# Re-timing the background transfers of a two-stage kernel: stores on GpSimd's queue, later weight casts, an earlier start

## The chip, the cores and the metric

The kernel runs on one core of a Trainium2 chip. The metric is device time in microseconds; quoted times are medians over several runs. The runs of one set were made on one chip, different sets on different chips, and times are compared only with runs of the kernel before on the same chip. A profile is one execution. "Gate end" below is the end of the last TensorE matmul of the first stage in the profile, counted from the start of the span.

## The reference, cut to what matters

```python
# gate loop: q, k, v, a_re, a_im are (4 batches, 8 heads, 768 steps, 48)
mag = np.sqrt(a_re * a_re + a_im * a_im)
scale = np.minimum(mag, 0.999) / (mag + 1e-06)
a_re_n, a_im_n = (a_re * scale, a_im * scale)
for t in range(S):
    ...   # S_re, S_im turned and shrunk by (a_re_n, a_im_n)
    S_re, S_im = (new_re + kv, new_im)
    y[:, :, t] = np.einsum('bhd,bhde->bhe', q[:, :, t], S_re)

# experts: x is y as 3072 rows of 384; 8 experts of 384 x 1024 x 384
logits = x @ w_gate + modality_bias[modality_id]
e_idx = np.argmax(logits, axis=1)
...       # gate_w is the softmax value of the chosen expert
h = np.maximum(x[mask] @ w1[e], 0.0)
out[mask] = gate_w[mask, None] * (h @ w2[e])
```

## The kernel before

The gate stage works on 24 units, one for each stretch of 128 steps of each batch, two units to a group. For a group, ScalarE and VectorE turn `a` into angles and moduli. For a unit, TensorE transposes Q and K, makes scores (`wp`), updates a state, makes outputs and turns them into rows. One loop runs the phases of several units in a software pipeline. A turn `w` belongs to one unit; negative turns fill the pipeline.

In the background, GpSimd's queue copies the experts' weights to bfloat16 in 16 "casts" of 768 KB output each. They are spread over the turns by hand. SyncE's queue carries everything else, in order: the loads of q, k, v and a; the stores of fractions (`f_scr`), moduli (`m_scr`) and rows (`x_rows`); the reloads of the fractions as carries (`cb`) and of the moduli (`mt`).

```python
    def moduli(x):
        ...
            nc.sync.dma_start(out=m_scr[n0:n0 + NG]..., in_=pm[L - 1:L, 0]...)
            mt = un.tile([C, NG, H], F32, name="mt", bufs=4)
            for c in range(2):
                nc.sync.dma_start(out=mt[c * D:(c + 1) * D], in_=m_scr[n0:n0 + NG].rearrange("i h d -> d i h"))
    ...
    phase(fractions, 0)
    phase(squares, 2)
    ...
    for w in range(-4, NU + 1):
        even = w % 2 == 0
        x = w // 2
        unit(values, w + 2)
        if even:
            phase(load_a, x + 6)
            phase(carries, x + 4)
            phase(fractions, x + 3)
        else:
            phase(load_qk, x + 3)
            hats(w + 3)
        unit(turned, w + 2)
        ...
        if w == 0:
            rt = make_router(ctx, ps, bank)       # loads the modality ids; VectorE compares them at once
        marks.append(chain[-1])
        if casts and w >= 0 and w % 3 != 2:
            cast = casts.pop(0)()                 # not before a mark two turns back
            tc.add_manual_dep(cast.ins, marks[-3].ins.name, ..., reason="spreads the casts over the turns")
```

After the gate stage come the router's last steps and the expert stage, which streams expert weights and does the two matmuls for up to 19 blocks of rows.

## Time and profile before

| measure, kernel before | value |
|---|---|
| median before the prediction, 3 runs | 396.49 us (395.16 to 397.88) |
| profiled execution, span | 392.2 us |
| scores of units 0, 2, 3, 5 start | 47.5, 68.6, 78.3, 96.6 us |
| scores of units 10 and 12 start | 145.9 and 171.8 us |
| gate end | 277.8 us |
| from there to the end of the span | 114.5 us |

The unit starts are read from TensorE's timeline. Where nothing disturbs it, a unit takes 9.75 us. So the table can be read as a sum: the ramp up to unit 5, the dip between units 10 and 12, a fixed pace, and the expert stage.

The waits of TensorE between 30 and 100 us (line waited for: total us, times, longest), which show the ramp hanging on ScalarE:

```profile
PE u L157 <- ACT tan L91: 14.7, 2, 9.7
PE wp L273 <- DVE f L180: 1.3, 2, 0.8
```

Second, GpSimd's timeline at 45 to 60 us (start, duration, what, and the idle time before it with what ended it). The first two casts start 7 us apart:

```profile
50.67 0.97 POOL L423 DMA_DIRECT2D w1b<-in_moe_w_dram  x1 [43.99 <-ACT off L91]
57.67 0.89 POOL L424 DMA_DIRECT2D w2b<-in_moe_w_dram  x1 [6.02 <-ACT sq L91]
```

The durations there are those of issuing. The page's list of transfers gives the landing: 7.6 us and 10.6 us after the issue, in the median. So the two overlap or touch, in the middle of the ramp.

### The profile page before, as it was taken

The page shows a single profiled execution, that of the slowest core. Times are in us where ns is not written, and L with a number is a line of the kernel's source. Part 1 is how long each engine was busy: PE and PEld are TensorE (multiplying, and loading weights), DVE is VectorE, ACT ScalarE, POOL GpSimd, SP SyncE. Part 2 cuts the span into 40 slices and gives each one's busy share as a digit, 9 for nine tenths or more (in the row PEclk, how much of TensorE's full clock was granted, in tenths as well). Part 3 has the DMA queues.
Part 4 walks back from the last instruction along what each step waited for, and adds up shares of the span by engine and source line. Part 5 has one row for each costly group of instructions (what it writes and reads, how often), then busy time and mean ns, then how long its engine had stood idle before and what let it go on. Part 6 is the DMA issues. An engine that isn't in the chain of part 4 may idle for free.

```text
span 392.2 us, 8756 instructions
## 1 busy us (share of the span) xinstructions
PE 328.1 (84%) x3381; PEld 269.9 (69%) x3381; DVE 259.0 (66%) x556; ACT 239.2 (61%) x386; POOL 79.6 (20%) x106
## 2 busy tenths in 40 slices
PE   0070949999999997899999999999407999999993
PEld 0030728788888886797979798999305777787772
DVE  2568797797969787997889789735632443443431
ACT  2859896989897978397979675352121333333331
POOL 5000010000000000000000011000045676776433
PEclk9996879999999999899999999999855999999999
DMA  9997599899899999979899993930169999999981
GB/s 145 187 152 173 91 163 184 125 195 195 150 222 159 184 166 217 185 126 147 184 181 186 153 160 64 185 69 13 30 245 365 404 404 413 405 407 406 411 357 40
DMA packets 173075, 80.89 MB, mean 206 GB/s; under 512 B 150387, under 2 KB 162152, under 8 KB 173034
## 3 DMA queue, kind: packets, MB, share of 16 engines
q1 hardware_dynamic: 158042, 59.97, 62.5%
q0 software_dynamic: 14992, 20.37, 26.5%
q8 instruction: 26, 0.43, 0.4%
q14 instruction: 15, 0.12, 0.1%
HBM read 85.75 MB, written 21.11 MB: 272 GB/s over the span
## 4 chain that ended last, share of the span: by engine, by line
PE 57%; ACT 11%; DMA 10%; issue 8%; POOL 4%; SPq 4%; DVE 4%; POOLq 0%; DVEq 0%; ACTq 0%
PE wp L273 9%; PE h_ps L702 7%; PE y_ps L713 6%; PE up L287 5%; PE xw L312 5%; PE yp L299 4%; DMA cb<-f_scr 4%; PE tQT L262 4%; PE yp L302 4%; PE tKT L262 4%; PE ls L207 4%; ACT sq L91 3%; PE u L157 3%; POOL out_dram L721 3%; ACT pm L91 2%
## 5 line engine op out<-in xcount | busy, mean ns | idle before, releaser
L157 PE MATMUL u<-tan,turn 128*128 128x384 f32 x48 | 24.4, 595 | 36.5 <-ACT tan L91 36.5
L273 PE MATMUL wp<-QT,KT 96*64 96x128 f32 x768 | 48.0, 278 | 1.7 <-DVE f L180 1.7
L273 PEld LDWEIGHTS wp<-QT,KT 96*64 96x64 f32 x768 | 42.2, 139 | 6.2 <-DVE f L180 2.7
L706 ACT ACTIVATE hT<-h_ps 128x512 bf16<-128x512 f32 x31 | 18.5, 597 | 45.6 <-PE h_ps L702 45.6
L702 PE MATMUL h_ps<-xgT,w1t 128*128 128x256 bf16 (+1 forms) x456 | 45.8, 259 | 0.0
L713 PE MATMUL y_ps<-w2t,hT 128*128 128x384 bf16 x248 | 43.5, 326 | 0.2 <-DVE hT L704 0.2
L702 PEld LDWEIGHTS <-w1t 128*128 128x128 bf16 x456 | 39.0, 100 | 5.9
L423 POOL DMA_DIRECT2D w1b<-in_moe_w_dram x8 | 5.9, 734 | 171.1 <-ACT off L91 86.3
L679 POOL DMA_INDIRECT xg<-x_rows,idx x31 | 30.0, 966 | 51.9 <-ACT idx L663 42.8
L157 PEld LDWEIGHTS u<-tan,turn 128*128 128x128 f32 x48 | 9.7, 230 | 41.2 <-issue 24.4
L721 POOL DMA_INDIRECT out_dram<-y_sb,idx x31 | 31.2, 1007 | 29.7 <-ACT y_sb L717 20.0
L299 PE MATMUL yp<-W,V 128*64 128x128 f32 x384 | 36.3, 277 | 0.0
L274 DVE TENSOR_TENSOR W<-wp,mask 128x512 f32<-128x512 f32 x48 | 32.3, 684 | 4.4 <-PE wp L273 4.3
L713 PEld LDWEIGHTS <-hT 128*128 128x128 bf16 x248 | 23.4, 98 | 14.1 <-DVE hT L704 0.3
L88 ACT ACT_TABLE_LOAD x25 | 32.1, 1283 | 1.2 <-PEq L800 0.8
L287 PEld LDWEIGHTS up<-V,Kh 128*96 128x96 f32 x320 | 29.5, 165 | 4.0 <-issue 2.7
L704 DVE TENSOR_SCALAR hT<-h_ps 128x512 bf16<-128x512 f32 x31 | 21.4, 692 | 16.0 <-PE h_ps L702 10.9
L302 PE MATMUL yp<-QT,state 96*48 96x128 f32 x320 | 31.1, 272 | 0.0
L287 PE MATMUL up<-V,Kh 128*96 128x48 f32 x320 | 30.4, 248 | 0.0
L263 ACT COPY KT<-tKT 96x512 f32<-96x512 f32 x48 | 25.8, 587 | 6.2 <-PE tKT L262 6.1
L304 ACT COPY yT<-yp 128x512 f32<-128x512 f32 x24 | 14.0, 585 | 22.7 <-PE yp L302 22.6
L312 PE MATMUL xw<-sel,yT 128*128 128x104 f32 x192 | 27.1, 285 | 0.0
(137 smaller groups left out, 653.3 us busy)
## 6 DMA issues: line engine op xcount, KB each, us to landing
w1t<-w1b SPq DMA_DIRECT2D x19, 768.0 KB, 12.0
w2t<-w2b SPq DMA_DIRECT2D x19, 768.0 KB
w1b<-in_moe_w_dram POOLq DMA_DIRECT2D x8, 768.0 KB, 7.6
w2b<-in_moe_w_dram POOLq DMA_DIRECT2D x8, 768.0 KB, 10.6
ab<-in_a_re_dram SPq DMA_DIRECT2D x24, 192.0 KB, 4.3
ab<-in_a_im_dram SPq DMA_DIRECT2D x24, 192.0 KB, 7.5
qk<-in_q_dram SPq DMA_DIRECT2D x24, 192.0 KB, 4.4
qk<-in_k_dram SPq DMA_DIRECT2D x24, 192.0 KB, 5.7
```

The lines of the kernel that those rows point to most:

```text
L88: then(nc.scalar.preload_act_table_set(name))
L157: nc.tensor.matmul(u, turn[:], tan[:, i], start=True, stop=False)
L262: nc.tensor.transpose(tp[:, i, :], src[:, h4 + i].rearrange("t c d -> t (c d)"), ident[:])
L273: nc.tensor.matmul(wp[u * 64:(u + 1) * 64, i, :], KT[:, h4 + i, u * 64:(u + 1) * 64], QT[:, h4 + i, :], start=True, stop=True)
L274: nc.vector.tensor_tensor(W[:, h4:h4 + 4], wp, mask[:, None, :].broadcast_to([L, 4, L]), Alu.mult)
L287: nc.tensor.matmul(up[:, h, :], Kh[:, h].rearrange("t c d -> t (c d)"), V[:, h, 0:D], start=True, stop=True)
L299: nc.tensor.matmul(yp[u * 64:(u + 1) * 64, j, :], V[:, 2 * j + u, :], W[:, 2 * j + u, :], start=True, stop=(g == 0))
L302: nc.tensor.matmul(yp[u * 64:u * 64 + D, j, :], old[:, 2 * j + u, :], QT[:, 2 * j + u, :], start=False, stop=True)
L312: nc.tensor.matmul(xw[:, j, :], yT[:, j, :], sel[:, j, :], start=True, stop=True)
L702: nc.tensor.matmul(h_ps[:, f, :], w1t[:, k, ff * 128:(ff + 1) * 128], xgT[:, k, :], start=(k == 0), stop=(k == KD - 1))
L713: nc.tensor.matmul(y_ps[:], hT[:, f, s * 128:(s + 1) * 128], w2t[:, f, :], start=(f == 0), stop=(f == NF - 1))
L721: sc = nc.gpsimd.indirect_dma_start(out=out, out_offset=bass.IndirectOffsetOnAxis(ap=idx[:, s, 1:2], axis=0), in_=y_sb[:], in_offset=None, ...
```

## The change

The intent is to keep TensorE from starving early in the gate stage: fewer weight casts while the loads are dense, no stores in front of loads in SyncE's queue, and the first units started one turn sooner. The diff, cut to its core:

```diff
-    Vs = [... for i in range(3)]
+    Vs = [... for i in range(4)]
...
-            nc.sync.dma_start(out=f_scr...)
+            nc.gpsimd.dma_start(out=f_scr...)
...
-            nc.sync.dma_start(out=m_scr...)
+            nc.gpsimd.dma_start(out=m_scr...)
...
-            for c in range(2):
-                nc.sync.dma_start(out=mt[c * D:(c + 1) * D], in_=m_scr...)
+    def decays(x):            # first half of mt, from memory
+            nc.sync.dma_start(out=mt[0:D], in_=m_scr...)
+    def decays2(x):           # second half, from the first, on the chip
+            nc.sync.dma_start(out=mt[D:C], in_=mt[0:D])
...
-        nc.sync.dma_start(out=x_rows...)
+        queue = nc.gpsimd if g < G - 1 else nc.sync
+        queue.dma_start(out=x_rows...)
...
-    phase(squares, 2)
+    with tc.issue_after(box["last"].ins):     # VectorE: after the first fractions
+        phase(squares, 2)
...
-        unit(values, w + 2)
+        n = w + 1 if w < 0 else w
+        unit(values, n + 2)
...      # likewise turned, inner, outer, hats, rows: n in place of w; each runs once
+            if w == -3:
+                hats(0)
...
+            if w < 0:
+                phase(sums, x + 2)
+                phase(moduli, x + 2)
...
-        if casts and w >= 0 and w % 3 != 2:
+        if casts and (w > 9 or w % 3 == 1 and w > 0):
```

More of the change, by code (lines that the diff above doesn't have):

```diff
@@ L72, in bank @@
         return flat.rearrange(f"p ({names}) -> p {names}", **{f"x{i}": s for i, s in enumerate(shape[1:])})
-    Vs = [un.tile([L, H, 64], F32, name=f"V{i}", bufs=1) for i in range(3)]
+    Vs = [un.tile([L, H, 64], F32, name=f"V{i}", bufs=1) for i in range(4)]
     for V in Vs:
@@ L185, in fractions @@
                 nc.vector.tensor_scalar(r[:, i], us[i], ROUND, -ROUND, Alu.add, Alu.add)
-                nc.vector.tensor_tensor(f[:, i], us[i], r[:, i], Alu.subtract)
+                box["last"] = nc.vector.tensor_tensor(f[:, i], us[i], r[:, i], Alu.subtract)
         if g < G - 1:
             n0 = g * B + b
-            nc.sync.dma_start(out=f_scr[n0:n0 + NG].rearrange("i c -> (i c)")[None], in_=f[L - 1:L].rearrange("o i h d -> o (i h d)"))
+            nc.gpsimd.dma_start(out=f_scr[n0:n0 + NG].rearrange("i c -> (i c)")[None], in_=f[L - 1:L].rearrange("o i h d -> o (i h d)"))
         nc.vector.tensor_scalar(r[:].bitcast(I32), f[:].bitcast(I32), 0x7FFFFFFF, None, Alu.bitwise_and)
@@ L221, in moduli @@
             n0 = g * B + b
-            nc.sync.dma_start(out=m_scr[n0:n0 + NG].rearrange("i h d -> (i h d)")[None], in_=pm[L - 1:L, 0].rearrange("o i h d -> o (i h d)"))
+            nc.gpsimd.dma_start(out=m_scr[n0:n0 + NG].rearrange("i h d -> (i h d)")[None], in_=pm[L - 1:L, 0].rearrange("o i h d -> o (i h d)"))
+        box["pm", x] = pm
+    def decays(x):
+        g, b = groups[x][0]
+        if g < G - 1:
+            n0 = g * B + b
             mt = un.tile([C, NG, H], F32, name="mt", bufs=4)
-            for c in range(2):
-                nc.sync.dma_start(out=mt[c * D:(c + 1) * D], in_=m_scr[n0:n0 + NG].rearrange("i h d -> d i h"))
+            nc.sync.dma_start(out=mt[0:D], in_=m_scr[n0:n0 + NG].rearrange("i h d -> d i h"))
             box["mt", x] = mt
-        box["pm", x] = pm
+    def decays2(x):
+        if ("mt", x) in box:
+            mt = box["mt", x]
+            nc.sync.dma_start(out=mt[D:C], in_=mt[0:D])
     def both(x):
@@ L232, in hats @@
     def hats(w):
-        if not 0 <= w < NU:
+        if not 0 <= w < NU or (hats, w) in done:
             return
+        done.add((hats, w))
         x, i = w // NG, w % NG
@@ L250, in values @@
     def values(g, b):
-        V = Vs[(g * B + b) % 3]
+        V = Vs[(g * B + b) % 4]
         nc.sync.dma_start(out=V[:, :, 0:D], in_=at(v, g, b))
@@ L281, in outer @@
         Kh, QT, W = box.pop(("inner", g, b))
-        V = Vs[(g * B + b) % 3]
+        V = Vs[(g * B + b) % 4]
         old = state.get(b)
@@ L316, in rows @@
         n0 = 1 + (b * G + g) * L
-        nc.sync.dma_start(out=x_rows[n0:n0 + L, 0:H * D // 2], in_=xr.rearrange("t j c -> t (j c)").bitcast(U32))
+        queue = nc.gpsimd if g < G - 1 else nc.sync
+        queue.dma_start(out=x_rows[n0:n0 + L, 0:H * D // 2], in_=xr.rearrange("t j c -> t (j c)").bitcast(U32))
     NX = len(groups)
@@ L332, in unit @@
     def unit(stage, w):
-        if 0 <= w < NU:
+        if 0 <= w < NU and (stage, w) not in done:
+            done.add((stage, w))
             stage(*order[w])
@@ L368, in gate_loop @@
             phase(carries, x + 4)
+            phase(decays2, x + 1)
             phase(fractions, x + 3)
@@ L371, in gate_loop @@
             phase(load_qk, x + 3)
-            hats(w + 3)
-        unit(turned, w + 2)
+            phase(decays, x + 2)
+            hats(n + 3)
+            if w == -3:
+                hats(0)
+        unit(turned, n + 2)
         if even:
@@ L380, in gate_loop @@
             phase(arctans, x + 4)
-        unit(inner, w + 1)
+        unit(inner, n + 1)
         if even:
@@ L387, in gate_loop @@
             late.clear()
-        unit(outer, w)
+        unit(outer, n)
         if even:
-            hats(w + 3)
+            hats(n + 3)
             phase(tangents, x + 4)
@@ L394, in gate_loop @@
             phase(squares, x + 5)
-        unit(rows, w - 1)
+        unit(rows, n - 1)
         if not even:
```

## The prediction

> **What bounds the kernel now.** I read the page first, then busy time by stretches, then the chain of waits, the timelines of TensorE, ScalarE and the SyncE queue, and last that queue's own waits. The page's second part shows two stages: a gate stage up to about slice 27 (275 us) and an expert stage after a gap.
>
> ```profile
> PE   0070949999999997899999999999407999999993
> ...
> PEclk9996879999999999899999999999855999999999
> DMA  9997599899899999979899993930169999999981
> ```
>
> The expert stage (280 us on) streams weights at 404 to 413 GB/s with DMA at 9 tenths; nothing in the diff touches it. So the question is when the gate stage ends. In it TensorE has idle slices only up to slice 5 and a dip at slices 14 to 16, with a lowered clock in slices 3 to 5. The stretches put numbers on this (columns: length, then busy us and instructions of PE, PEld, DVE, ACT, POOL; granted clock; DMA share; GB/s):
>
> ```profile
> 20.00:60.00 40.00, 23.51 (x111) 15.36 (x112) 31.97 (x51) 33.55 (x45) 1.86 (x2) 0.79 0.88 146
> 60.00:100.00 40.00, 38.69 (x412) 32.33 (x411) 32.68 (x59) 34.22 (x54) 1.54 (x2) 1.00 1.00 169
> 100.00:140.00 40.00, 39.60 (x446) 34.09 (x444) 33.26 (x58) 33.95 (x53) 2.24 (x3) 1.00 1.03 185
> 140.00:180.00 40.00, 36.60 (x411) 31.86 (x411) 32.75 (x87) 31.09 (x49) 2.04 (x3) 0.96 0.98 165
> 180.00:220.00 40.00, 40.00 (x452) 34.70 (x450) 35.00 (x59) 33.91 (x54) 1.90 (x3) 1.00 1.01 177
> 220.00:260.00 40.00, 40.00 (x506) 36.01 (x506) 30.56 (x80) 21.26 (x40) 3.12 (x4) 1.00 0.79 133
> 260.00:280.00 20.00, 18.17 (x255) 16.79 (x250) 9.87 (x47) 7.03 (x15) 0.00 (x0) 1.00 0.15 36
> ```
>
> TensorE is the floor from 60 us on: 40.00 of 40 where nothing disturbs it. The timeline gives its pace: the scores (wp) of successive units start at 191.3, 201.1, 210.8, 220.6 and 230.3 us, 9.75 us a unit. DMA is the second limit, full up to 220 us and nearly empty at the end (0.15). The dip is one wait (start, duration, engine, idle before):
>
> ```profile
> 151.20 1.14 PE L312 MATMUL xw<-sel,yT 128*128 128x104 f32 x8
> ...
> 154.35 0.51 PE L262 MATMUL tKT<-ident,Kh 128*96 128x128 f32 x3
> 158.11 0.17 PE L547 MATMUL rank<-acc,ones 128*128 128x8 bf16 x1 [3.26 <-DVE acc L526]
> ```
>
> The chain of waits tells what held VectorE then: the load of the carries, behind the SyncE queue's loads.
>
> ```profile
> 147.51 1.07 SPq L106
> 148.57 0.04 issue
> 148.62 8.72 DMA cb<-f_scr
> 157.39 0.04 issue
> 157.43 0.56 DVE f L180
> ```
>
> The queue itself loses time to stores and slow issues (waits: total us, times, longest):
>
> ```profile
> SPq L252 <- PE yp L302: 18.2, 5, 5.8
> SPq L317 <- ACT xr L315: 16.5, 9, 4.5
> ...
> SPq L225 <- DMA m_scr<-pm: 7.7, 6, 2.2
> ```
>
> **What the Trainium skill says.** "DMA: Bandwidth & Descriptors", section "Issuing engines are not separate DMA queues", says that DMAs of all issuers share the same 16 engines, and that another issuer saves only sequencer time. The trace agrees as far as it can: the stores issue in 0.25 to 0.4 us each, so their move buys no bandwidth, only the end of the waits just shown. The same page, "Rules for kernel authors", says that a strided last dimension becomes one descriptor per element. The trace sorted by packet size has 22,341 packets of 4 bytes on the hardware queue; 20 loads of the moduli at 768 elements are 15,360 of them. "SBUF — State Buffer", in its box on the "DVE blocks DMA" trap, says that VectorE in a two-port mode can lock GpSimd out of writing descriptors. The casts land here in 7.6 and 10.6 us beside a VectorE that is 82% busy, so I see no large effect, but no row isolates it. "TensorE: Matmul & The Clock Gate", Part 1, says the default clock is half and activity releases it; here it was half at 32.5 to 42.8 and 53.0 to 59.8 us, both after idle stretches.
>
> **The change, part by part.**
>
> Casts. Before, 7 of 16 are issued in turns 0 to 9; after, 3 (turns 1, 4, 7), then one in each turn from 10 to 22. With the other queue silent at 240 to 260 us, two casts filled the engines for 9.9 us, so 5 us each. A load of q, k, v or a has 1,024 packets of 192 bytes; at 0 to 30 us the queue moved 25,759 packets, so about 1.2 us a load. A pair of early turns asks for 10 such loads (12 us), the carries (1.3 us), moduli (15,360 packets x 10 ns / 16 / 10 groups = 1 us) and rows (0.6 us): 15 us. Casts in two of three turns add 6.7, so 21.7 us against TensorE's 19.5 a pair: DMA loses 2.2 us a pair for five pairs, about 11 us. The lead of the prefetched buffers hides some, and the rest breaks out as the dip at 154 us. With casts in one of three turns it is 15 + 3.3 - 0.5 = 17.8, below 19.5. So the early shortage goes, and with it the dip. Its size: units 10 to 12 start at 145.9 and 171.8, 25.9 us for 19.5. About 0.9 us of the surplus of 6.4 are the router's own matmuls, so 5.5 us are to be had.
>
> Late turns. Two casts a pair are 10 us, six loads 7.2, carries 1.3, the rest 1: 19.5, exactly TensorE's pace. The first such pair still loads a (24 us), but a buffered group of lead (one pair) covers 5 us. From turn 16 the carries and then q and k end. So no loss, without margin.
>
> Stores by GpSimd, fourth value buffer. These free SyncE of most of 16.5 + 7.7 us of waits and part of 18.2. None is on TensorE's path by itself after 170 us; they count as security for the carries: 0 us alone. Moduli copied on chip: 768 instead of 1,536 tiny elements a group, 0.5 us of DMA a pair, counted above.
>
> Units moved up. ScalarE sets the ramp. Before, its copies of the transposed Q and K (four of 0.5 us a unit) end at 45.0, 52.3, 61.4, 71.4, 79.2 and 89.4 us for units 0 to 5. Two edits help. The squares of group 2 no longer stand ahead of the first fractions on VectorE, whose delay ScalarE shows as 4.22 us:
>
> ```profile
> 27.99 0.84 ACT L91 ACTIVATE cs<-f 128x768 f32<-128x768 f32 x1 [4.22 <-DVE f L186]
> ```
>
> Without two 0.95 us products, an addition and a 0.55 us compare among them, the sine starts at about 26.3. Then from the built order: second sine 28.5, table 29.9, moduli 31.4, logs and exponents 34.6, table 35.9, and copies of unit 0, with an arctangent between, until 38.9. Adding tables at 1.28, sines 1.6, squares 1.45, four moduli 1.5, copies 2.1 in the new order gives the ends 44.2, 54.4, 66.2, 74.5 and 83.4 for units 1 to 5: 6.0 us before the old ones at unit 5, if ScalarE never waits. TensorE, starting at 36 instead of idling to 38.5 and from 49.5 to 54.5, needs about 8.8 us a unit here and can follow. I count 6 us. The small waits of TensorE on VectorE before the scores of units 3, 5 and 7 (0.80, 0.50, 0.40 us) partly go: 1 us.
>
> Sum: 5.5 + 6 + 1 = 12.5 us, less 0.5 for new waits. 396.5 - 12 = 384.5; I say 384.
>
> **The rivals.** First, the late casts take back what the early turns gain. The stores share GpSimd's queue with casts, and a row store behind a 10 us cast holds one of two row buffers. For it: the balance of 19.5 against 19.5, and three casts that hang on the same last ScalarE instruction. Against it: DMA share 0.15 after 260 us, two turns of slack for each store, and q and k loaded well ahead. It would cost 4 to 8 us: 388 to 392. Second, ScalarE or VectorE becomes the bound. A steady pair is about 18 us on ScalarE (33.9 of 40 in a steady stretch) and 17.5 on VectorE, so neither reaches 19.5, but in the ramp both are nearly full, and a waiting pair of them could eat half the 6 us: 387. Third, TensorE was starved less than it seems and the dip only moves to the second router step: then just the ramp, 389 to 390. Fourth, fuller success: the clock stays up from 43 us on and TensorE's pace holds at 8.8 us through the first units, giving 8 us in the ramp: 381.
>
> **Range and chances.** Rival 1 and 3 give the upper end, 4 the lower with the spread of the runs (395.2 to 397.9) on top: 377 to 391. Faster by over 2% means below 388.6, which needs 8 of the 12 us: 0.77. Within 2%: 0.21. Slower: 0.02, as that needs rival 1 far beyond its estimate.
>
> **What would show it.** Right: scores of unit 5 start at 89 to 91 us (before 96.6); units 10 to 12 stay near 9.75 us apart, no TensorE wait over 1 us between 100 and 200 us; DMA share below 1 in 60 to 140 us and above 0.9 in 200 to 250; last matmul of the gate at about 265 us (before 277.8); the expert stage still some 114 us from there. Wrong: a TensorE or ScalarE wait after 150 us released by a DMA, or by row stores; a last cast that lands after the router's result and holds the first weight load; unit 5 not earlier than 94 us.

## The result, and the profile after

Ratios in this document are the mean time of one kernel's runs over that of the other's of the same rounds, so they are not quite the ratio of the medians quoted.

| measure | before | after |
|---|---|---|
| median on the first chip, 4 runs each | 395.83 us (392.72 to 397.88) | 383.93 us (383.44 to 384.35) |
| ratio, with its 95% interval | | 0.971 (0.964 to 0.977) |
| scores of unit 5 start | 96.6 us | 90.8 us |
| units 10 to 12 | 25.9 us | 20.6 us |
| gate end | 277.8 us | 266.2 us |
| from there to the end of the span | 114.5 us | 115.6 us |

The changed kernel is 11.9 us faster in the median. The two profiled executions differ by 10.5 us, since that of the kernel before (393.93 us) was faster than three of its four timed runs. In them the gate stage ends 11.6 us sooner: 5.8 us by unit 5, 0.5 us from there to unit 10, and 5.3 us between units 10 and 12. From unit 12 to unit 23 both kernels take 97.0 us.

The page of the changed kernel shows the dip of TensorE gone. The clock in the ramp is lowered less: 7 tenths and 8 tenths in slices 3 and 5, where it had been 6, 8 and 7 in slices 3 to 5:

```profile
PE   0074889899999999999999999998219999999991
...
PEclk9997989999999999999999999999558999999997
```

The same stretches as before, from the changed kernel (length, busy us and instructions of PE, PEld, DVE, ACT, POOL; granted clock; DMA share; GB/s):

```profile
20.00:60.00 40.00, 29.26 (x184) 21.04 (x185) 32.91 (x54) 35.53 (x48) 4.07 (x6) 0.87 0.92 147
60.00:100.00 40.00, 38.65 (x408) 32.79 (x407) 37.92 (x65) 37.52 (x60) 6.87 (x10) 1.00 1.04 185
...
140.00:180.00 40.00, 40.00 (x465) 34.67 (x463) 36.93 (x94) 33.81 (x54) 7.95 (x13) 1.00 0.97 164
```

TensorE gained 5.75 us of busy time at 20 to 60 us and 3.4 us at 140 to 180 us. DMA stayed as full as it was: the change did not empty the transfer engines, it changed what stood in them at which moment. From 60 to 140 us the share of GpSimd's queue fell from 36.9% to 21.2% of the engines' time, and that of SyncE's queue rose from 64.1% to 77.1%. The waits of TensorE at 30 to 100 us, after:

```profile
PE tKT L273 <- DVE Kh L256: 8.8, 2, 5.2
PE u L157 <- ACT tan L91: 1.4, 1, 1.4
```

Of 16.0 us, 10.2 are left, and from 100 to 262 us no wait of TensorE is listed at all. Most of what is left in the ramp hangs on VectorE (`Kh`) and no longer on ScalarE: the scores of unit 1 came 8.2 us sooner than before, those of unit 3 only 5.2. The ramp's first landmark, in ScalarE's timeline, is the first sine (bracket: idle before it, and what ended it); it came at 27.99 us before:

```profile
26.71 0.84 ACT L91 ACTIVATE cs<-f 128x768 f32<-128x768 f32 x1 [2.80 <-DVE f L186]
```

GpSimd's queue now holds one cast where there were two, the next following 25 us later:

```profile
57.50 0.73 POOL L447 DMA_DIRECT2D w1b<-in_moe_w_dram  x1 [10.07 <-ACT sq L91]
...
82.20 0.88 POOL L448 DMA_DIRECT2D w2b<-in_moe_w_dram  x1 [1.94 <-ACT off L91]
```

And SyncE's queue has a new wait in place of old ones (total us, times, longest):

```profile
SPq L237 <- DMA mt<-m_scr: 27.6, 9, 7.8
...
SPq L330 <- ACT xr L326: 9.6, 4, 4.5
SPq L230 <- DMA m_scr<-pm: 7.7, 3, 3.8
...
SPq L263 <- PE yp L313: 3.5, 1, 3.5
```

Line 237 is the on-chip copy of the moduli, which must wait for the half that comes from memory. The longest single sum in this queue is therefore one that the change itself brought. It holds up loads that are ahead of need, so TensorE does not feel it; the experiments come back to it.

### The profile page after: what moved, and what is told of

Read it like the earlier page. It is cut to its first block, busy times and chain, and to the rows that moved or that the text cites. A ratio compares the mean times of both kernels' runs of the same rounds, so it can differ in the third digit from the quotient of the medians.

```text
span 381.7 us, 8805 instructions
## 1 busy us (share of the span) xinstructions
PE 325.4 (85%) x3381; PEld 268.9 (70%) x3381; DVE 260.0 (68%) x556; ACT 238.8 (63%) x386; POOL 104.7 (27%) x147
## 4 chain that ended last, share of the span: by engine, by line
PE 68%; issue 8%; ACT 8%; POOL 5%; DMA 4%; SPq 3%; DVE 2%; POOLq 1%; DVEq 0%; ACTq 0%
PE wp L284 11%; PE up L298 7%; PE h_ps L726 7%; PE xw L323 6%; PE y_ps L737 6%; PE yp L310 6%; PE tQT L273 5%; PE tKT L273 5%; PE yp L313 5%; PE ls L207 4%; PE u L157 3%; POOL out_dram L745 3%; ACT sq L91 2%; POOL xg L703 2%; DMA xg<-x_rows,idx 1%
## 5 line engine op out<-in xcount | busy, mean ns | idle before, releaser
L157 PE MATMUL u<-tan,turn 128*128 128x384 f32 x48 | 22.7, 559 | 23.3 <-ACT tan L91 23.3
L273 PE MATMUL tKT<-ident,Kh 128*96 128x128 f32 x192 | 26.4, 281 | 8.8 <-DVE Kh L256 8.8
L273 PEld LDWEIGHTS tKT<-ident,Kh 128*96 128x96 f32 x192 | 21.9, 131 | 12.0 <-DVE Kh L256 5.8
L330 POOL DMA_DIRECT2D x_rows<-xr x20 | 12.9, 643 | 56.4 <-ACT xr L326 56.4
## 6 DMA issues: line engine op xcount, KB each, us to landing
w2b<-in_moe_w_dram POOLq DMA_DIRECT2D x8, 768.0 KB, 10.2
```

Of the source, the lines that this page charges most:

```text
L157: nc.tensor.matmul(u, turn[:], tan[:, i], start=True, stop=False)
L273: nc.tensor.transpose(tp[:, i, :], src[:, h4 + i].rearrange("t c d -> t (c d)"), ident[:])
```

## The experiments

The total had come out as predicted, so the question was whether its parts had. My theory was that of the prediction: the casts make the dip (about 5 us), the units moved up make the ramp (about 6 us), and the stores and buffers are worth about 0 alone. The rivals were that the stores' move, which the change makes everywhere, is what lets the carries arrive; and that the parts depend on each other, so that no list of separate gains exists.

Two things are needed to read the results. First, two of the chips run the expert stage slower in every kernel that was profiled there: the changed kernel itself took 134.9 us from the gate end there and 115.6 on the first chip. The windows 300 to 320 us of the first chip's profile of the changed kernel:

```profile
300.00:320.00 20.00, 20.00 (x182) 15.41 (x179) 8.73 (x15) 7.28 (x13) 14.38 (x15) 1.00 1.02 408
```

and of the same kernel's second profile, on a slower chip:

```profile
300.00:320.00 20.00, 16.54 (x150) 11.73 (x148) 6.76 (x11) 5.21 (x9) 11.68 (x12) 1.00 1.00 373
```

DMA engines with nearly the same busy share moved 373 instead of 408 GB/s and TensorE idled. In one kernel on that chip (a_casts_old) the same 20 us show 410 GB/s, and TensorE idled all the same. So why the stage is slower there stays open; it may be the chip, or something else that ran on it. The gate stage was the same: 266.0 us here, 266.2 there. So I compare gate ends across chips, and times only within one. Second, from unit 10 to 13 every kernel without a dip takes 30.4 us; their gate ends differ only by stalls and by the ramp. The summary, gate figures from the profiles:

| kernel | unit 5 | 10 to 12 | gate end | median | before, same chip |
|---|---|---|---|---|---|
| before | 96.6 | 25.9 | 277.8 | | |
| changed, run again (a_rerun) | 90.7 | 20.6 | 266.0 | 402.73 | 413.34 |
| changed, old cast turns (a_casts_old) | 97.2 | 25.6 | 277.5 | 411.24 | 413.34 |
| changed, units not moved up (a_units_old) | 92.8 | 20.6 | 268.2 | 405.68 | 413.34 |
| changed, stores on SyncE (a_stores_old) | 90.7 | 20.6 | 267.3 | 403.00 | 413.34 |
| before, new cast turns (b_casts_new) | 95.2 | 20.6 | 273.1 | 391.08 | 393.86 |
| before, units moved up (b_units_new) | 98.1 | 20.6 | 276.0 | 392.73 | 393.86 |
| before, stores on GpSimd (b_stores_new) | 101.6 | 20.6 | 277.0 | 399.15 | 393.86 |
| changed, one cast moved from turn 7 to 0 (a_casts_014) | 98.8 | 20.6 | 274.2 | 391.78 | 393.86 |
| changed, old cast turns, router later (a_old_router4) | 91.0 | 20.6 | 274.2 | 412.00 | 413.83 |
| before, new cast turns and stores (b_casts_stores) | 95.5 | 20.6 | 270.8 | 407.22 | 413.83 |
| changed, squares unordered (a_no_hint) | 92.3 | 20.6 | 267.6 | 404.54 | 413.83 |
| changed, old V buffers and moduli (a_v3_mt) | 90.3 | 20.6 | 265.6 | 401.95 | 413.83 |

### The changed kernel again

No edit. It gives the reference for its chip.

> The changed kernel again, as the reference of this group. Every theory: about 384 us, ratio to the kernel before near 0.970; scores of unit 5 start near 91 us, units 10 to 12 start 20.6 us apart, last matmul of the gate stage near 266 us.

Measured: 402.73 us against 413.34, ratio 0.977 (0.972 to 0.981); gate end 266.0. The gate end repeats to 0.2 us; the kernel before was not profiled on this chip. The ratio is nearer to 1. The longer expert stage explains little of that: the first chip's 11.7 us (difference of the means) would be a ratio of 0.972 here, but the means differ by 9.8 us. The two intervals overlap, and where the rest went is not shown.

### Old cast turns in the changed kernel

```diff
-        if casts and (w > 9 or w % 3 == 1 and w > 0):
+        if casts and w >= 0 and w % 3 != 2:
```

> The changed kernel with the old spacing of the casts (two of three turns from turn 0). Theory A (the casts spent the DMA engines' time that the carries needed): the ramp keeps its gain (unit 5 near 91 us), but a stall of TensorE behind the carries comes back between units 8 and 13, some 5 us, so about 389 us. Theory B (the carries were late because SyncE's queue stood behind the stores, which are now elsewhere): no stall, 384 to 385 us. As the changed kernel also has half the tiny elements of the moduli to load, A may be a little less than 5 us.

Measured: 411.24 us, ratio 0.999 (0.994 to 1.004): the whole gain is gone with this one line. Gate end 277.5. The dip came back as expected (25.6 us for units 10 to 12), but the ramp was lost too: unit 5 at 97.2. The waits at 55 to 100 us:

```profile
DVE is_m L508 <- DMA mid<-in_moe_modality_id_dram: 5.7, 1, 5.7
...
PE u L157 <- ACT tan L91: 4.4, 1, 4.4
```

and at 145 to 180 us:

```profile
DVE tan L121 <- DMA ab<-in_a_im_dram: 6.0, 1, 6.0
...
PE up L298 <- DVE own L573: 2.9, 1, 2.9
```

In both, VectorE's queue, which runs in order, stops at an instruction that waits for a transfer, and TensorE starves behind it. The first is an odd one: `is_m` compares the modality ids for the router, which nobody needs before unit 7 is done. It stops the ramp only because it stands in the queue (how it came to stand there is told at "Stores alone"). The second is a different load from the one of the kernel before (there it was the carries), at about the same place and of about the same size.

### Units not moved up in the changed kernel

```diff
-        n = w + 1 if w < 0 else w
+        n = w
-            if w == -3:
-                hats(0)
-            if w < 0:
-                phase(sums, x + 2)
-                phase(moduli, x + 2)
```

> The changed kernel with the first units at their old turns and the early moduli taken out; the order of VectorE's first fractions stays. Theory A (two independent gains): the ramp loses what the moved units brought, 6 us less the 1.3 us of the earlier first sine, so unit 5 near 95.5 us and 388.5 us in all, with no stall at units 10 to 12. Rival C (TensorE catches up later, because it is not the bound in the following units): below 386 us.

Measured: 405.68 us, 2.95 us over the changed kernel on this chip; ratio to before 0.984 (0.980 to 0.988). Unit 5 at 92.8, gate end 268.2. The edit's own loss is 2.2 us in the gate stage, well below what I expected. Moving the units up is not what made most of the ramp's 5.8 us.

### Stores back on SyncE in the changed kernel

```diff
-            nc.gpsimd.dma_start(out=f_scr...      # likewise m_scr and x_rows
+            nc.sync.dma_start(out=f_scr...
```

> The changed kernel with its stores of fractions, moduli and rows back on SyncE's queue, the rest as changed. Theory A: these waits are off TensorE's path, so 384 to 385 us and no stall over 1 us between 100 and 200 us. Theory B (the queue's waits for stores delay the carries): the stall at units 10 to 12 is back, 388 to 390 us.

Measured: 403.00 us against 402.73 for the changed kernel, equal within their spread (one of its six runs was slow, 411.10); gate end 267.3. The rival that the stores carry the gain falls for this structure. Of the 1.3 us in the gate stage, 1.0 is one wait of TensorE on VectorE late in the stage.

### New cast turns alone in the kernel before

```diff
-        if casts and w >= 0 and w % 3 != 2:
+        if casts and (w > 9 or w % 3 == 1 and w > 0):
```

> The kernel before with nothing changed but the turns of the casts (1, 4, 7, then every turn from 10). Theory A2, formed after the first four runs: the DMA time of the early casts is nearly the whole matter, in the ramp too. Then the scores of unit 5 start at about 93 us (96.6 before), units 10 to 12 are 20 to 21 us apart and the last matmul of the gate comes near 269 us (277.8 before), 8 to 9 us off. The theory on record (casts 5.5, units 6): unit 5 still at 96.6, gate end at 272.

Measured: 391.08 us against 393.86, ratio 0.997 (0.992 to 1.003). The gate end, 273.1, missed my 269. The dip is gone, but the ramp hardly moved (95.2), and new waits of TensorE came late. At 170 to 262 us:

```profile
PE ls L207 <- ACT xr L315: 1.5, 1, 1.5
PE up L287 <- ACT xr L315: 0.9, 1, 0.9
```

This is the first rival of the prediction, on a small scale: late casts take 2.5 us of TensorE's time near units 15 and 20. VectorE, on which those copies hang, had itself waited for loads of q and k. The same wait list for the changed kernel is empty. So the late casts do bite in this kernel, whose stores still stand in SyncE's queue. The stores are not all of it: the changed kernel with its stores back on SyncE has late casts too, and lost only 1.0 us to a wait there.

### Units moved up alone in the kernel before

```diff
-        unit(values, w + 2)
+        n = w + 1 if w < 0 else w
+        unit(values, n + 2)      # and the rest of the moved units, as in the change
```

> The kernel before with only the first units moved up and the early moduli. Theory A2: with the casts still in turns 0 and 1 it brings under 1.5 us, gate end 276 to 278, although ScalarE's early copies come sooner. The theory on record: 4.7 us (6 less the 1.3 of the order on VectorE), gate end 273, unit 5 near 92 us.

Measured: 392.73 us against 393.86, ratio 1.000 (0.996 to 1.005). The start was gained and lost again: unit 3 stood at 75.7 us, 2.6 us ahead, and unit 5 at 98.1, 1.5 us behind. The waits at 80 to 115 us:

```profile
DVE f L180 <- DMA cb<-f_scr: 5.8, 1, 5.8
...
PE wp L274 <- DVE f L180: 4.6, 1, 4.6
```

These are the carries, which stalled the kernel before at 151 us. Here they hold VectorE at about 91 to 97 us; units 5 and 6 start 13.5 and 12.3 us after the ones before them, and units 10 to 12 run undisturbed. The dip did not vanish; it was paid sooner.

### Stores alone in the kernel before

```diff
-            nc.sync.dma_start(out=f_scr...      # likewise m_scr and x_rows
+            nc.gpsimd.dma_start(out=f_scr...
```

> The kernel before with only the stores of fractions, moduli and rows moved to GpSimd. Theory A2: within 1.5 us of the kernel before, the stall at units 10 to 12 stays. Theory B (SyncE's queue stood behind its stores): the stall goes, gate end near 272.

Measured: 399.15 us against 393.86, ratio 1.016 (1.012 to 1.021). Both theories missed: it is slower. The profile fell on the fastest of its runs (395.46), so it shows less than the usual loss: gate end 277.0, expert stage 2.3 us longer than before. What it does show is the stall moved once more, to units 1 to 2. The first line is from the waits at 55 to 80 us, the second from SyncE's timeline:

```profile
DVE is_m L485 <- DMA mid<-in_moe_modality_id_dram: 7.4, 1, 7.4
```

```profile
54.03 6.51 SPq L460 DMA_DIRECT2D mid<-in_moe_modality_id_dram  x4
```

The four id loads, of 6 KB each, took 6.5 us to issue while two casts were under way, and VectorE stopped at the compare for 7.4 us. In the kernel before, the same four loads took 2.7 us to issue, and 15 us later:

```profile
69.00 1.24 SPq L459 DMA_DIRECT2D mid<-in_moe_modality_id_dram  x2
```

So the edit moved more than the stores. When the program is built, instructions are put in order for each queue, and in all four kernels with the stores on SyncE the id loads begin at 67 to 70 us and the compare waits 0.1 to 2.7 us for them. With the stores on GpSimd, and the router's constants in turn 0, the id loads begin at 51 to 54 us. There the compare waits 7.4, 5.7 and 8.7 us when casts stand in turns 0 and 1 (this kernel, a_casts_old and the next one), and not at all with the new cast turns, b_casts_stores among them. The stall of this kernel's ramp thus comes from that order together with the two early casts.

Why the median loss is larger than the profiled run's stays open; the six slower runs show a lower granted clock (0.928 to 0.932 against 0.940).

### One cast in turn 0 in place of turn 7

The two experiments so far in which the compare of the ids holds up the ramp have casts in turns 0 and 1. This kernel keeps the number of casts before turn 10 at three, as in the changed kernel, and moves one of them.

```diff
-        if casts and (w > 9 or w % 3 == 1 and w > 0):
+        if casts and (w > 9 or w in (0, 1, 4)):
```

> The changed kernel with its three early casts in turns 0, 1 and 4 in place of 1, 4 and 7; the late ones as they are. Theory A2 with two separate stalls: the one in the ramp comes back (units 2 to 3 over 14 us apart in place of 10.5, unit 5 at 95 to 97 us), the one at units 10 to 13 does not, gate end 270 to 272 (266 as changed). Rival: only the number of casts before turn 10 counts, then gate end 266 to 267.

Measured: 391.78 us against 393.86, ratio 0.996 (0.991 to 1.001); the changed kernel had 0.971 on the first chip, whose expert stage takes as long as this one's. Gate end 274.2, which is 8.2 us later than the changed kernel's 266.0. So one cast moved by seven turns gives back most of the gain, though no more bytes move before turn 10. The stall came back in the ramp alone, as expected, but larger: 8.2 us where 270 to 272 against 266 had meant 4 to 6. SyncE's timeline shows it; the two issues are the two halves of the moduli:

```profile
50.82 0.33 SPq L230 DMA_DIRECT2D mt<-m_scr  x1
...
58.16 0.53 SPq L237 DMA_DIRECT2D mt<-mt  x1
```

and in the changed kernel:

```profile
50.84 0.33 SPq L230 DMA_DIRECT2D mt<-m_scr  x1
...
53.45 0.53 SPq L237 DMA_DIRECT2D mt<-mt  x1
```

The first half, 3 KB in tiny pieces, was issued at the same moment in both. With a cast issued 0.4 us ahead of it the copy could be issued 7.0 us after the first issue had ended, without it 2.3 us. SyncE's queue runs in order, and three of the four id loads stand behind the copy. But this wait is not the whole cause. In a_casts_old the cast stood just as close ahead, the copy came after 3.2 us, and the stall was there all the same: the three id loads behind it took 5.3 us to issue, against 2.8 in the changed kernel. The next lines, of VectorE and of TensorE, show the stall going on to the path that sets the end:

```profile
68.14 0.18 DVE L508 TENSOR_SCALAR is_m<-mid 128x24 f32<-128x24 int32 x1 [8.70 <-DMA mid<-in_moe_modality_id_dram]
```

```profile
75.13 1.65 PE L157 MATMUL u<-tan,turn 128*128 128x384 f32 x2 [7.38 <-ACT tan L91]
```

### Old cast turns, with the router's constants four turns later

If the ids are just the first thing in the way, taking them out of the way should bring the ramp back, and the debt should appear elsewhere.

```diff
-        if casts and (w > 9 or w % 3 == 1 and w > 0):
+        if casts and w >= 0 and w % 3 != 2:
-        if w == 0:
+        if w == 4:
             rt = make_router(ctx, ps, bank)
```

> The changed kernel with the old spacing of the casts, and the router's constants (the loads of the modality ids and what VectorE makes of them) built in turn 4 in place of turn 0. Theory A3: the shortage of DMA time is paid once, at whatever waits first. With the ids out of VectorE's way in the ramp, unit 3 follows unit 2 within 12 us (16.3 with the old casts alone), but the later stall behind the loads grows to 7 us or more, and the gate stage still ends at 274 to 278 us. Rival D: the two stalls are separate, each with its own waiter. Then the first is gone for good and the gate stage ends at 270 to 272.

Measured: gate end 274.2. The ramp came back in full (unit 5 at 91.0 against 90.8), and unit 6 came 17.6 us after it instead of 9.8. The wait moved with the ids, which VectorE now meets in turn 4:

```profile
DVE is_m L508 <- DMA mid<-in_moe_modality_id_dram: 9.7, 1, 9.7
```

In this kernel too a cast stood just ahead of the first half of the moduli, and the copy came 7.1 us after it; with no id loads behind it, the ramp did not feel it. So what costs the ramp is what stands behind in the queue, and the long wait alone does no harm there. I had expected the later stall, at units 11 to 12, to grow and the gate to end at 274 to 278 us; the gate end just fits, but the stall was still that of the ids. No second dip followed, so 3.3 us of the loss of the old turns were saved. The time, 412.00 us, is not to be read against its chip's before. That kernel scattered there from 406.99 to 418.13 us, and the rule that calls a run slow at 1.5% over the fastest left three of its eleven runs. The ratio, 1.007 (1.000 to 1.014), uses those three alone.

### New cast turns and stores together in the kernel before

```diff
-            nc.sync.dma_start(out=f_scr...      # likewise m_scr and x_rows
+            nc.gpsimd.dma_start(out=f_scr...
-        if casts and w >= 0 and w % 3 != 2:
+        if casts and (w > 9 or w % 3 == 1 and w > 0):
```

> The kernel before with the new turns of the casts and the three kinds of stores on GpSimd, nothing else. Theory A3: with the casts late, SyncE's queue has to bring q, k and v beside one cast a turn, and there its waits for stores show: casts alone lost 2.6 us at units 14 to 21. Without them the gate stage ends near 270 us (273 with the casts alone) and the ratio is near 0.980. If the stores do nothing, 273 and 0.99.

Measured: gate end 270.8, as expected; 407.22 us against a median of 413.83, where the ratio is 0.995 (0.987 to 1.003) for the reason just given. The late waits of the kernel with the new cast turns alone are gone: its list of TensorE's waits at 170 to 262 us is empty. So the stores' move, harmful alone in this structure, is worth 2.3 us of the gate stage once the casts are late (1.3 us in the changed kernel).

### The squares left unordered in the changed kernel

```diff
-    with tc.issue_after(box["last"].ins):
-        phase(squares, 2)
+    phase(squares, 2)
```

> The changed kernel without the order of VectorE's first fractions before the squares of group 2. As on record: the first sine starts 1.3 us later (28.0 in place of 26.7 us), gate end about 267.3, total 1 to 1.5 us longer. If another engine sets the ramp: under 0.5 us.

Measured: 404.54 us; gate end 267.6, unit 5 at 92.3. The first sine is at 28.15 us, 1.4 us later than with the order. This small part is worth 1.4 to 1.6 us, not much less than moving the units up (2.2 us).

### Three value buffers, moduli loaded twice, in the changed kernel

```diff
-    Vs = [... for i in range(4)]
+    Vs = [... for i in range(3)]
-            nc.sync.dma_start(out=mt[D:C], in_=mt[0:D])
+            nc.sync.dma_start(out=mt[D:C], in_=m_scr...)
```

> The changed kernel with three value buffers and with both halves of the moduli loaded as single elements again. As on record: 0.5 us of DMA time a pair more, all of it beside other work, so under 1 us in all; gate end 266 to 267. SyncE's queue loses its wait for the first half (27.6 us in nine times) and gains waits for value buffers. If these buffers or elements matter: over 2 us and a stall after unit 14.

Measured: 401.95 us; gate end 265.6 against 266.0 and 266.2. These two parts of the change are worth nothing here. It was not timed on one chip with the changed kernel, so I do not call it the better one. One more part was never tested alone: the change also issues the loads of the moduli one to two turns later than before, and this kernel keeps that.

### What follows from all of them

The four kernels with the old cast turns and the router's constants in turn 0 end the gate stage at 277.8, 277.5, 276.0 and 277.0 us. What else was changed in them only decides where the stall falls: at units 10 to 12, at 2 to 3 and again 11 to 12, at 4 to 6, or at 1 to 2. The seven kernels with the new turns end it between 265.6 and 273.1, whatever else was varied. That fits the picture of a debt of transfer time, paid at whichever queue first reaches a transfer that is late. Two kernels lie between, both at 274.2: three early casts with one in turn 0, and the old turns with the ids out of the way. So the sum of bytes alone does not set the debt. The parts are not additive in the gate stage: casts alone 4.7 us, units alone 1.8, stores alone 0.8, all together 11.6 (which has the order of the squares, the buffers and the later moduli in it too).

It is not settled how the debt splits between engines that are full and SyncE's queue waiting in front of loads that could have gone. The DMA share is at 0.9 to 1.0 in both kernels, and the kernel with a cast in turn 0 shows that place counts beside volume. An experiment that keeps one and varies only the other was not found. Each gate end is also from one profile; kernels with stalls vary by several microseconds between runs.

## Why the prediction was right

The total was right: 384 predicted, 383.93 measured. That it fits to a tenth is luck: the base moved from 396.5 to 395.83, and errors in the parts partly cancel. Point by point:

- TensorE as the floor at 9.75 us a unit, the early casts' load on DMA as the cause of the dip, and an untouched expert stage held. The gate end was predicted at about 265 and measured at 266.2; the expert stage took 115.6 us where 114 was said.
- The dip, 5.5 us predicted, gave 5.3. Undoing the casts alone brought it back.
- The ramp, 6 us predicted, gave 5.8 at unit 5. The ends of ScalarE's copies came within 1.2 us of the list: 39.2, 44.1, 54.3, 67.4, 75.2 and 84.2 us.
- The small waits before units 3, 5 and 7, 1 us predicted, are all gone (1.7 us). But 1.3 of these lie in the ramp and are part of its 5.8 us; the new cast turns alone remove them (unit 5 at 95.2 in place of 96.6). Without them the ramp gave 4.5 us, not 6: that term was too large and this one too small. ScalarE's copies of unit 5 came 5.2 us sooner, not 6.0.
- Stores, fourth buffer and on-chip copy at 0 alone held in the changed kernel (0.3 us in the median for the stores). As a part added to the kernel before, the stores were not 0: 1.6% slower; in the profile the ids' compare, brought forward, stalled the ramp. Of SyncE's waits that they were to end, 16.5 us fell to 9.6; the 7.7 us are those of the load of the moduli for its store, and stayed 7.7.
- Rival 1, that late casts take back the gain, was rightly put aside for the whole change. It is real in the kernel before with the new cast turns alone: 2.5 us.
- Rival 2, a pair of VectorE and ScalarE that waits in the ramp, came true in part: TensorE's waits for `Kh` there are 8.8 us. Its sum was off: 33.9 of 40 us is 16.5 us a pair on ScalarE, not 18. The conclusion for the steady stretch stands.

One term was wrong in its cause: "Units moved up", with "I count 6 us". I worked out ScalarE's new order and assumed that ScalarE never waits. That assumption is not a property of the moved units. It holds only if no queue on the way stops for a late load: either the casts of turns 0 and 1 are not both there, or the ids' compare is out of the way, as in a_old_router4, which has both casts and still reaches unit 5 at 91.0 us (and pays at unit 6). With the units moved up and the old casts, unit 5 stands at 97.2 us, later than the 96.6 of the kernel before. With the new casts and the units not moved, it stands at 92.8. So of the 5.8 us, moving the units is worth 2.0 given the rest, and the order of the squares 1.5; undoing the casts costs 6.4, more than the whole.

The bookkeeping of DMA time was also weaker than it looked. It said 17.8 us of transfers for 19.5 us of work after the change, which is a share of 0.91, and a share below 1 from 60 to 140 us. Measured there were 0.99 (1.04 to 100 us, then 0.94), against 1.02 before: the sign held, by little. The other queue, called silent at 240 to 260 us, moved 3,520 packets then; the 5 us for a cast stand, as the 9.9 us are the casts' own packet time. The count gave the right sign and a fair size for the dip, but it treats a turn as a bin, and which turn a cast stands in proved to matter beside the count.

## What to carry to other kernels

When background transfers compete with loads that in-order queues wait for, the place of a large one matters beside their number: look for the small transfers issued just after it and for whatever stands behind them in each queue. Read the order from the trace: an edit that moves stores to another queue can move other instructions too, as it did with the ids' compare here. A stall that moves instead of vanishing points to a debt; undo one part at a time in the changed kernel as well as adding one part to the old, since for the casts the two answers were 11.5 and 4.7 us of the same stage. A load for later use should not have its first consumer early in a busy engine's queue.

## What the Trainium skill lacked or had wrong

- "DMA: Bandwidth & Descriptors", section "Issuing engines are not separate DMA queues", says that another issuer saves only sequencer time, usually small beside the transfer. For bandwidth the runs agree: in the changed kernel the stores' move is worth 0.3 us in the median. What it lacks is the order of waiting: the same stores moved alone made the kernel 1.6% slower, with four id loads 15 us earlier in SyncE's queue, and together with later casts they took 2.3 us off the gate stage. The sequencer's time was not always small either: these four loads of 6 KB took 6.51 us to issue there, and 2.7 us in the kernel before.
- The same page, section "Queues, rings and completion order", says that a transfer engine takes turns between the queues it has work for, packet by packet. One would expect a 3 KB load to pass beside a cast with little delay. It gives no figure for this; here the wait behind such a load was 7.0, 7.1 and 3.2 us with a cast issued just ahead and 2.3 us without.
- Nothing was lacking or wrong, as far as the runs show, on two pages that the prediction used. "TensorE: Matmul & The Clock Gate", Part 1: the trace agrees that idleness costs clock; the mean granted clock at 20 to 60 us rose from 0.79 to 0.87 with less idle time. "SBUF — State Buffer", box on the "DVE blocks DMA" trap: no run here isolates it. GpSimd had many more transfers to describe after the change and the changed kernel still showed no late wait of TensorE.
